# Counting 96-row and 96-column products as full-size ones in a kernel that orders its own work by a clock in the source

## The chip, the cores and the metric

The kernel runs on one core of a Trainium2 chip. Its time is the device time of one launch in microseconds (us), as the median of several runs; lower is better. Short names for engines: PE is TensorE (matmul), PEld its weight loads, DVE is VectorE, ACT is ScalarE, POOL is GpSimd, SP is SyncE, which here only starts DMAs.

## The reference

For x of 2048 tokens and 576 channels, the output is g * a + (1 - g) * b. Here g is a sigmoid of x times a gate vector, a is a long convolution (a state-space layer of 128 states for each channel), and b is a mixture of 4096 tiny experts chosen by product keys in 32 heads:

```python
P = jnp.exp(logdA[:, :, None] * l[None, None, :])
K = jnp.einsum("dn,dnl,dn->dl", Cc, P, dB).real
...                                    # y = irfft(rfft(u) * rfft(K)) + u * Dskip
q = jnp.einsum("nd,dhc->nhc", xf, w_q)             # 32 heads, 2 x 128
s1 = jnp.einsum("nhd,ed->nhe", q1, k1)             # 64 scores, and s2 alike
i1 = jnp.argsort(-s1, axis=-1)[..., :K]            # best 2 of 64, and i2 alike
...                                    # best 2 of the 4 pairs, softmax g
act = _gelu(jnp.einsum("nd,nhkd->nhk", xf, ue))
out = jnp.einsum("nhk,nhk,nhkd->nd", g, act, ve)
```

## The kernel before

All the work is in one function, `body`, written out as one long stream of instructions. Each engine executes its own instructions in the order in which the source issues them, so that the order of issue is the schedule. Exact f32 products are made of three f16 products (high and low halves).

**The work.** In the first two thirds PE works through 128 *s groups* and 128 *a groups*. An s group (`s{c}_{t}`, c 0 to 7, t 0 to 15) makes 512 scores for 128 tokens in 14 products of 128x512; DVE then searches each of its 8 pieces of 64 scores with MAX8 (`m`) and FIND_INDEX8 (`i`), 16 instructions. An a group (`a{c}_{tb}_{j}`) multiplies 128 experts by 512 tokens in 14 products; ACT or DVE empties it into `go`, which SP stores to `g_d`. The operands are built as it goes: `whl` and `wb` from the query weights and keys, `uhl` and `wrem` of each of 8 expert chunks (loaded as `us` and `ur`), each a scaled copy on ACT or DVE and a remainder on DVE.

Beside these groups other pieces run. `k_front` and `k_gen` build the convolution's kernel in 36 steps, two at a time: `k_front` makes angles on PE, `kP`, as two products with 96 rows (and for every fourth step `k_factors` makes their 96-column operand `wbp`), reduces them to `CS` on ACT or DVE, and takes exponents (`e`, `ex`) and sines on ACT; `k_gen` multiplies them (`Y`, `e` on DVE) and makes the tile `kb` in small products of 32 columns. This is called the k stage; it lasts from about 110 to 600 us. `u_stage1` transforms the tokens in 32 steps: ACT and DVE split `uh`, PE makes `u1`, and SP stores it. Then `products` multiplies the two transforms (`ki`, `ui` loaded; `pr`, `pi` on PE; `tt`, `vf`, `vo` on DVE, ACT and POOL; `pv` on PE), `v_work` splits the experts' second matrix into `vhl`, `gating` turns the searches into weights, and `prep` spreads them over experts by one-hot products (`A`, `Be`, `Bg`, then `S`) into the weight tile `wh`. From about 1017 us on PE makes the output tiles `o` from `wh` and `vhl`, 192 products for each of 16 token tiles.

**What sets the order.** The source keeps a count of time of its own while it issues, `clock[0]`. Only `mm` and waiting advance it. Each side piece is a Python generator that yields how long it wants to wait; `pump` resumes those that are due by the count, between PE's groups and every third product inside one. An object for each of DVE, ACT and POOL (`V`, `S`, `G`) adds up when that engine will be free by estimated durations; `rdy` keeps when each tile will be ready. The count of PE's time stands in `mm` (lines 206 to 213):

```python
    def mm(o, l, r, start, stop, cost=None):
        m = l.shape[0], size(l)
        if m != tiling[0]:
            tiling[0] = m
            clock[0] += 0.15 if m == (128, 128) else 0.1
        clock[0] += (size(r) * (4 if r.dtype == F32 else 1) / 2400 + 0.003) if cost is None else cost
```

`m` is the shape of the stationary operand: rows (the contraction) and columns. The count is read in many places. The main loop (line 1534 on) chooses between the next s group and the next a group by how far DVE is behind:

```python
        lag = V.free - clock[0]
        ...
        a_ok = a_ok and (len(acts) > 26 or not groups)
        ...
        if groups and bank_free() and lag < (6.0 if not a_ok else 2.0 if not turn_s else 5.0 if kdone[0] < NCK else 8.0):
```

The last 26 a groups are held back until no s group is left. `k_front` chooses ACT or DVE for each reduction of kP by `S.free <= V.free` (lines 709 and 718 on), `act_post` for each emptying of an a group by `S.free <= V.free + 0.5`. `u_build` (line 1184) starts to load an expert chunk c once `adone[0]`, the a chunks done, has reached c, or c - 1 while the k stage runs or the s groups are not near their end:

```python
        while adone[0] < c - (kdone[0] < NCK or sdone[0] >= 7):
```

In the profile nearly all instructions of DVE, ACT and POOL have line 133 (the engine object), DMAs have line 204 and matmuls line 213, so that one goes by the names of the tiles.

## Time and profile before

| | |
|---|---|
| median of 3 runs | 1479.43 us (1478.44 to 1482.02) |
| profiled execution: time, and span | 1478.13 us, 1476.3 us |
| mean granted clock of PE | 0.995 |
| PE busy | 1434.3 us, 97% |
| DVE / ACT / POOL busy | 1254.2 / 786.0 / 537.7 us |
| chain that ended last | PE 73%, DVE 19%, DMA 3% |

Busy time is the union of an engine's instructions. A chain is followed back from the last instruction, at each step to what released it. PE is nearly always busy, so what is read below is where it is not, and who released it there.

### The profile page before, as it was taken

To read this page: it belongs to the slowest core of one execution; us is meant where nothing else is said; L and a number is where in the kernel's file an instruction comes from. 1 tells how busy PE (TensorE), PEld (TensorE's weight loads), DVE (VectorE), ACT (ScalarE), POOL (GpSimd) and SP (SyncE) were. 2 spreads that over 40 slices of the span, in tenths; PEclk is the share of its full clock that TensorE was granted. 3 is DMA by queue.
4 is the path that set the end of the run, shared out by engine and by line. 5 is a ranking of instruction groups with operands and counts; after the bars stand their busy time and mean duration, and the time that the engine had idled before them with its cause. 6 is when DMAs were issued, how large, how long until landed. Compare 5 with 4: busy or idle time off the path is not lost.

```text
span 1476.3 us, 36780 instructions
## 1 busy us (share of the span) xinstructions
PE 1434.3 (97%) x14024; PEld 861.1 (58%) x14028; DVE 1254.2 (85%) x4589; ACT 786.0 (53%) x1310; POOL 537.7 (36%) x513
## 2 busy tenths in 40 slices
PE   5999999999999999999999999999999999999999
PEld 3444544454455544555554444456787788788787
DVE  6989899989988899598997997589998998898860
ACT  6558778677686866625655644664424324323310
POOL 0454663634726465202247999522010110110100
PEclk9999999999999999999999999999999999999999
DMA  6443542443344343466576758676532442442400
GB/s 227 133 121 103 173 129 76 151 134 94 107 130 147 108 133 122 132 218 234 177 269 228 267 192 258 208 245 186 191 119 92 131 144 70 151 146 67 154 9 17
DMA packets 139184, 221.20 MB, mean 150 GB/s; under 512 B 11648, under 2 KB 82688, under 8 KB 132608
## 3 DMA queue, kind: packets, MB, share of 16 engines
q1 hardware_dynamic: 138912, 218.78, 46.2%
q8 instruction: 110, 1.80, 0.5%
q14 instruction: 66, 0.54, 0.1%
q10 hardware_dynamic: 96, 0.07, 0.0%
HBM read 147.51 MB, written 71.30 MB: 148 GB/s over the span
## 4 chain that ended last, share of the span: by engine, by line
PE 73%; DVE 19%; DMA 3%; ACT 2%; issue 2%; SPq 0%; POOL 0%; DVEq 0%; ACTq 0%
PE o L213 23%; PE a L213 19%; PE s L213 17%; DVE i L133 4%; PE S L213 4%; DVE m L133 3%; PE wb L213 2%; DVE e L133 2%; PE kb L213 2%; DVE uhl L133 2%; PE pr L213 1%; DVE Y L133 1%; DVE CS L133 1%; PE y L213 1%; DVE uh L133 1%
## 5 line engine op out<-in xcount | busy, mean ns | idle before, releaser
L213 PE MATMUL o<-vhl,wh 128*128 128x288 f16 x3072 | 387.3, 286 | 0.0
L213 PE MATMUL s<-whl,xb 128*128 128x512 f16 x1536 | 366.4, 381 | 5.9 <-DVE whl L133 3.5
L213 PE MATMUL a<-xb,uhl 128*128 128x512 f16 x1536 | 362.4, 380 | 4.1 <-DVE i L133 4.1
L213 PEld LDWEIGHTS <-wh 128*128 128x128 f16 x3072 | 295.9, 98 | 76.4 <-issue 3.7
L213 PEld LDWEIGHTS <-xb 128*128 128x128 f16 x1792 | 171.4, 98 | 211.4 <-issue 20.8
L213 PEld LDWEIGHTS <-uhl 128*128 128x128 f16 x1536 | 147.9, 98 | 178.7 <-issue 5.7
L133 DVE FIND_INDEX8 i<-m,s 128x8 uint32<-128x64 f32 x1024 | 206.5, 223 | 0.0
L133 ACT ACTIVATE wh<-gl,s_wg 128x1024 f16<-128x1024 f32 x63 | 67.6, 1137 | 206.8 <-DVE gl L133 206.8
L133 DVE MAX8 m<-s 128x8 f32<-128x64 f32 x1024 | 146.3, 215 | 24.6 <-PE s L213 23.3
L133 POOL TENSOR_TENSOR CS<-CS,ex 128x512 f32<-128x512 f32 x72 | 100.6, 1427 | 153.5 <-DVE ex L133 144.3
L133 POOL TENSOR_TENSOR ya<-ya,db 128x576 f32<-128x576 f32 x16 | 31.8, 1994 | 341.2 <-DVE Bg L133 151.2
L133 DVE SCALAR_TENSOR_TENSOR wh<-gl,s_wg,wh 128x1024 f16<-128x1024 f32 x64 | 90.6, 1447 | 11.3 <-ACT wh L133 11.3
L133 DVE TENSOR_TENSOR gl<-S,gl 128x256 f32<-128x256 f32 x256 | 90.0, 415 | 10.2 <-PE S L213 9.2
L133 POOL TENSOR_TENSOR e<-aN,rt 128x512 f32<-128x512 f32 x72 | 86.4, 1221 | 31.8 <-PE kb L213 31.7
L133 ACT ACTIVATE go<-a,i_a 128x512 f32<-128x512 f32 x95 | 64.4, 683 | 52.1 <-PE a L213 35.2
L133 DVE TENSOR_TENSOR Bg<-Be,vals 128x1024 f16<-128x1024 f16 x128 | 89.6, 741 | 2.2
L133 ACT ACTIVATE gl<-gl 128x1024 f32<-128x1024 f32 x64 | 63.5, 1045 | 44.8 <-DMA gl<-g_d 41.4
L133 DVE TENSOR_TENSOR A<-iota_a,vals 128x2048 f16<-128x2048 f16 x64 | 79.9, 1249 | 0.0
L213 PE MATMUL s<-wrem,xb 128*128 128x512 f16 x256 | 76.7, 381 | 0.1
L213 PE MATMUL a<-xb,wrem 128*128 128x512 f16 x256 | 76.2, 379 | 0.0
L213 PE MATMUL S<-Bg,A 128*128 128x64 f16 x2048 | 73.1, 193 | 2.6 <-DVE Bg L133 2.4
L213 PEld LDWEIGHTS <-A 128*128 128x128 f16 x2048 | 70.8, 97 | 7.7 <-issue 1.8
(202 smaller groups left out, 2225.2 us busy)
## 6 DMA issues: line engine op xcount, KB each, us to landing
g_d<-go SPq DMA_DIRECT2D x128, 256.0 KB, 2.5
gl<-g_d SPq DMA_DIRECT2D x32, 1024.0 KB, 5.7
wq<-in_wq_dram SPq DMA_DIRECT2D x16, 1152.0 KB, 7.1
us<-in_au_dram SPq DMA_DIRECT2D x64, 144.0 KB, 3.0
su_d<-us SPq DMA_DIRECT2D x32, 288.0 KB, 2.7
sk_d<-k1o SPq DMA_DIRECT2D x32, 288.0 KB, 3.0
vn<-in_vv_dram SPq DMA_DIRECT2D x32, 288.0 KB, 3.2
ui<-su_d SPq DMA_DIRECT2D x16, 576.0 KB, 4.2
```

The source lines that it names most:

```text
L133: return f(*a, **k)
L213: T.matmul(o, l, r, start=start, stop=stop)
```

## The change

`mm` counts a change of tiling only between classes: over 64 rows or not, and over 64 columns taken as 128. Products of 96 rows (kP) and of 96 columns (wbp) are so taken as full size. The charge for a return to full size goes from 0.15 to 0.13. No instruction's operands, shape or engine is named in it.

```diff
     def mm(o, l, r, start, stop, cost=None):
-        m = l.shape[0], size(l)
+        m = l.shape[0] > 64, 128 if size(l) > 64 else size(l)
         if m != tiling[0]:
             tiling[0] = m
-            clock[0] += 0.15 if m == (128, 128) else 0.1
+            clock[0] += 0.13 if m == (True, 128) else 0.1
```

PE has the same 11612 matmul instructions in both programs; their order differs from the first kP on. Two places are shown; a row is an instruction, its line, operation, written and read tiles (with buffer numbers), and shape.

On DVE, around the fifth pair of kb (about 230 us), before has both remainders uh9 and uh10 and the remainder of chunk 3 between the searches of score groups s1_8 and s1_9:

```order
L133 MAX_INDEX i8_1_8_2842<-m8_1_8_2841,s1_8_2818 128x8 x8
L133 TENSOR_TENSOR Y9_2866<-e9_2378,CS9_2383 128x1024
L133 TENSOR_TENSOR e9_2378<-e9_2378,CS9_2383 128x16x32
L133 SCALAR_TENSOR_TENSOR e9_2378<-e9_2378,CS9_2383 128x16x32
L133 COPY ex8_2348<-ex8_2348 128x2
L133 COPY ex9_2379<-ex9_2379 128x2
L133 SCALAR_TENSOR_TENSOR uh9_2760<-us_1119,sci_76,uh9_2760 64x576
L133 SCALAR_TENSOR_TENSOR uh10_2787<-us_1119,sci_76,uh10_2787 64x576
L133 SCALAR_TENSOR_TENSOR uhl3_2592<-us3_2469,sci_76,uhl3_2592 128x512
L133 MAX m8_1_8_2841<-s1_9_2926 128x8 x8
```

and now:

```order
L133 MAX m8_1_8_2910<-s1_10_2943 128x8 x8
L133 MAX_INDEX i8_1_8_2911<-m8_1_8_2910,s1_10_2943 128x8 x8
L133 TENSOR_TENSOR Y10_3074<-e10_2634,CS10_2639 128x1024
L133 TENSOR_TENSOR e10_2634<-e10_2634,CS10_2639 128x16x32
L133 SCALAR_TENSOR_TENSOR e10_2634<-e10_2634,CS10_2639 128x16x32
L133 TENSOR_TENSOR Y11_3078<-e11_2669,CS11_2674 128x1024
L133 TENSOR_TENSOR e11_2669<-e11_2669,CS11_2674 128x16x32
L133 SCALAR_TENSOR_TENSOR e11_2669<-e11_2669,CS11_2674 128x16x32
L133 COPY ex10_2635<-ex10_2635 128x2
L133 COPY ex11_2670<-ex11_2670 128x2
L133 SCALAR_TENSOR_TENSOR uh9_2894<-us_1119,sci_76,uh9_2894 64x576
L133 SCALAR_TENSOR_TENSOR uh10_2904<-us_1119,sci_76,uh10_2904 64x576
```

uh9 and uh10 moved behind the searches of s1_9 and s1_10 and behind the products of the k steps 10 and 11, a pair of steps later.

On SP, before loads expert chunk 7 (us7, ur7) among the loads of `products`:

```order
L204 DMA ki5_10478<-sk_d_67 128x1152
L204 DMA vn32_10546<-in_au_dram 32x576 x4
L204 DMA z_d_69<-vo2_10437 128x1152
L204 DMA us7_10627<-in_uT_dram 128x4x512
L204 DMA ur7_10628<-in_uT_dram 64x512 x2
L204 DMA vn33_10636<-in_au_dram 32x576 x4
L204 DMA ui6_10665<-su_d_66 128x1152
```

and now at the end of the k stage, ahead of the last store of a chunk 5:

```order
L204 DMA su_d_66<-us_1119 32x4x576
L204 DMA g_d_65<-go5_3_2_7455 128x4x128
L204 DMA us7_7469<-in_uT_dram 128x4x512
L204 DMA ur7_7470<-in_uT_dram 64x512 x2
L204 DMA g_d_65<-go5_3_3_7478 128x4x128
L204 DMA k_d_68<-ko_7580 128x1024
L204 DMA wq4_1_7655<-in_wq_dram 128x2304
L204 DMA ksb_7665<-k_d_68 128x18x256
L204 DMA g_d_65<-go6_0_0_7700 128x4x128
L204 DMA g_d_65<-go6_0_1_7721 128x4x128
L204 DMA g_d_65<-go6_0_2_7747 128x4x128
```

The load moved some 94 places up; behind it, ahead of the products, stand stores of a chunk 6 (go6_0_0 and on): six a groups of chunk 6 come there now that stood behind the last s group before. So 26 a groups are left behind the last s group, s7_15, where before had 31.

## The prediction
> **What bounds the kernel now.** I read the page first, then busy time by stretches, then the stretches where TensorE (PE) stands still.

> ```profile
> span 1476.3 us, 36780 instructions
> PE 1434.3 (97%) x14024; PEld 861.1 (58%) x14028; DVE 1254.2 (85%) x4589; ACT 786.0 (53%) x1310; POOL 537.7 (36%) x513
> ```

> PE is busy for 1434.3 of 1476.3 us, so 42.0 us is all that an order could bring, plus what the slowed clock costs; and the change leaves PE's products as they are. The windows say where those 42 us lie. The columns are the window, its length, busy time of PE, PE's weight loads, VectorE (DVE), ScalarE (ACT) and GpSimd (POOL), then granted clock, DMA share and GB/s.

> ```profile
> core 0: us, PE busy (x) PEld busy (x) DVE busy (x) ACT busy (x) POOL busy (x), PEclk, DMA share, GB/s
> 200.00:280.00 80.00, 72.84 (x701) 36.85 (x700) 78.75 (x305) 53.21 (x83) 49.56 (x36) 0.98 0.43 131
> 280.00:400.00 120.00, 118.61 (x1287) 61.41 (x1286) 109.18 (x465) 88.50 (x131) 62.14 (x51) 1.00 0.38 116
> 400.00:480.00 80.00, 79.77 (x747) 40.98 (x746) 68.64 (x269) 59.42 (x91) 38.08 (x34) 1.00 0.42 131
> 480.00:560.00 80.00, 80.00 (x741) 39.86 (x740) 73.00 (x270) 62.08 (x88) 41.10 (x33) 1.00 0.42 126
> 560.00:640.00 80.00, 77.38 (x907) 41.02 (x905) 63.45 (x286) 47.85 (x79) 29.87 (x25) 1.00 0.47 150
> 800.00:910.00 110.00, 107.61 (x983) 51.06 (x980) 98.69 (x529) 56.53 (x150) 105.30 (x108) 0.98 0.73 240
> 214.24:217.66 3.42, 3.05 (x108) 2.81 (x111) 3.39 (x5) 0.00 (x0) 3.42 (x3) 0.50 0.56 151
> 849.12:852.54 3.42, 3.42 (x18) 1.19 (x10) 3.42 (x19) 1.66 (x4) 3.34 (x4) 0.50 0.84 275
> ```

> From 200 to 280 us PE stands still for 80.00 - 72.84 = 7.16 us while DVE has 78.75 of 80: DVE sets the pace there. From 280 to 640 it stands for 1.39 + 0.23 + 0.00 + 2.62 = 4.24, from 800 to 910 for 2.39. Two stretches of 3.42 us have a granted clock of 0.50; each costs at most half its length, 1.7 us. The timeline (start, duration, instruction, and in brackets PE's wait and who ended it) shows what the waits are:

> ```profile
> 214.19 0.44 PE L213 MATMUL kb<-Y,CS 128*32 128x64 f32 x8 [2.71 <-DVE i L133]
> 254.15 0.41 PE L213 MATMUL u<-uh,tu 128*128 128x288 f16 x2 [1.79 <-DVE uh L133]
> 255.90 0.41 PE L213 MATMUL u<-uh,tu 128*128 128x288 f16 x2 [0.66 <-DVE uh L133]
> 273.17 0.59 PE L213 MATMUL a<-xb,uhl 128*128 128x512 f16 x2 [1.62 <-DVE i L133]
> 584.13 0.39 PE L213 MATMUL a<-xb,uhl 128*128 128x512 f16 x1 [2.51 <-DVE i L133]
> 848.30 0.43 PE L213 MATMUL pi<-ui,cst 64*64 64x256 f32 x2 [1.60 <-DVE m L133]
> ```

> All six end on DVE; the four of 200 to 280 are 2.71 + 1.79 + 0.66 + 1.62 = 6.78 of the 7.16. PE reached an instruction whose operand or bank was still behind other work in DVE's queue. That is what an order can shift.

> **The change part by part.** *The count itself.* A count inside the source runs no engine; only the order that it sets can act. By the order, 60 products or groups enter a tiling of 96 rows or columns in before (51 of kP, 9 of wb): 60 x 0.1 = 6.0 us of count go, with 43 returns x 0.15 = 6.5; the 86 other returns fall by 0.02, 1.7 together. The count ends up 14.2 us shorter, nearly all of it while kP runs. Does the chip charge what was taken out?

> ```profile
> 281.67 0.81 PE L213 MATMUL s<-whl,xb 128*128 128x512 f16 x3
> 282.41 0.32 PE L213 MATMUL kb<-Y,CS 128*32 128x64 f32 x8
> 285.51 2.11 PE L213 MATMUL s<-whl,xb 128*128 128x512 f16 x9
> 287.45 0.60 PE L213 MATMUL kP<-rt,wb 96*128 96x512 bf16 x2
> 287.89 0.38 PE L213 MATMUL s<-whl,xb 128*128 128x512 f16 x1
> L213 PE MATMUL kP<-rt,wb x72: 377/381/390, 110.6 to 590.5; 96*128 96x512 bf16 x72
> ```

> Nine s products take 287.45 - 285.51 = 1.94, 0.216 each; the two kP products between the same neighbours take 287.89 - 287.45 = 0.44, 0.22 each: nothing for 96 rows. Into kb (32 columns) the three s products take 0.74 where 3 x 0.216 is 0.65: 0.09 for a real switch. So the new count is nearer to the chip. Real switches fall from 172 to 170 in the order: 2 x 0.09, under 0.2 us; I put 0.

> *k stage, 110 to 640 us.* With a shorter count DVE looks further behind PE, so what asks for DVE's lag (which of s and a goes next, whether ACT or DVE reduces a kP or empties an a) turns from DVE to ACT, and side work comes due after more matmuls. I counted each operation in the two orders between the first and the sixth pair of kb and priced it by DVE's groups of 110 to 640 us (count, busy us, mean ns):

> ```profile
> L133 DVE SCALAR_TENSOR_TENSOR uh<-us,sci,uh 64x576 f16<-64x576 f32 x32 | 44.7, 1413 | 1.5 <-ACT uh L133 0.8
> L133 DVE SCALAR_TENSOR_TENSOR CS<-CS,kP 128x512 f32<-128x512 f32 x49 | 32.6, 679 | 2.0 <-ACT CS L133 1.7
> L133 DVE TENSOR_SCALAR go<-a,i_a 128x512 f32<-128x512 f32 x25 | 18.3, 744 | 8.7 <-PE a L213 8.6
> L133 DVE TENSOR_TENSOR CS<-CS,kP 128x512 f32<-128x512 f32 x23 | 15.8, 687 | 0.8
> L133 DVE TENSOR_SCALAR CS<-kP 128x512 f32<-128x512 f32 x23 | 15.7, 683 | 6.4 <-PE kP L213 6.4
> L133 DVE TENSOR_SCALAR whl<-wb,sci 128x512 f16<-128x512 f32 x9 | 6.5, 745 | 7.4 <-PE wb L213 7.4
> ```

> and the short searches by the timeline, where they overlap (8 MAX8 in 1.15 us; a FIND_INDEX8 every 0.20):

> ```profile
> 227.64 1.15 DVE L133 MAX8 m<-s 128x8 f32<-128x64 f32 x8
> 228.76 0.24 DVE L133 FIND_INDEX8 i<-m,s 128x8 uint32<-128x64 f32 x1
> 228.96 0.23 DVE L133 FIND_INDEX8 i<-m,s 128x8 uint32<-128x64 f32 x1
> ```

> uh 10 to 8: -2 x 1.41 = -2.8. kP reduced on DVE alone 7 to 5, with ACT's help 13 to 15: -2 x (0.683 + 0.687) + 2 x 0.679 = -1.4. whl 3 to 0, at the 0.745 of its group: -2.2. go 4 to 3: -0.7. MAX8 8 and FIND_INDEX8 7 more: 1.15 + 7 x 0.20 = +2.6. Together -4.5, and with the groups too small to list -4.9. PE's own work between these marks, by its rows' spacing, is 121.7 us before and 120.7 after; DVE's is 122.0 and 117.1. So DVE goes from 0.3 over PE to 3.6 under. I take 4.5 of the 7.16, short of all since a single late operand still stops PE when the sums fit (bounds 0 and 7.2). The slow clock at 214 begins at the end of the 2.71 us wait; 1.2 of its 1.7 goes with it (bounds 0 and 1.7). For 280 to 640, where DVE has slack, I take 2.5 of 4.24: DVE's rows up to the 28th kb fall from 476.4 to 457.1 against PE's 494.1 to 485.5, 10.7 us more room, but at 584 a single hand-over is late and that can come back elsewhere (bounds 0 and 4.2).

> *Products, 800 to 910 us.* The load of expert chunk 7 stands earlier in SP's queue and its split moves out of here, into the end of the k stage:

> ```profile
> L133 DVE TENSOR_TENSOR tt<-tt 128x512 f32<-128x512 f32 x7 | 10.1, 1448 | 0.5
> L133 DVE SCALAR_TENSOR_TENSOR vhl<-vhl,sci,vhl 128x576 f16<-128x576 f32 x8 | 9.0, 1173 | 0.0
> L133 DVE SCALAR_TENSOR_TENSOR uhl<-us,sci,uhl 128x512 f16<-128x512 f32 x4 | 5.2, 1290 | 0.0
> L133 DVE SCALAR_TENSOR_TENSOR wrem<-ur,sci,wrem 64x512 f16<-64x512 f32 x1 | 1.2, 1202 | 0.0
> ```

> The four uhl and the wrem, 5.2 + 1.2 = 6.4 us of DVE, leave. Between the tenth and the nineteenth pr vhl also goes from 8 to 4 (-4.7), and two more each of the tt sums and vf products come in, 2 x (1.448 + 1.026) = +4.9; copies out of PSUM go to ACT and gating steps come in for about as much. By the order DVE's work there goes from 4.0 us over PE's (45.9 to 41.9) to 0.6 under (40.1 to 40.7). I take 2.8 of the 4.1 there (2.39 standing still, 1.7 slow clock; bounds 0 and 4.1). The load passes one store of a and, further on, the ui, ki and vn loads; a chunk of that size behind a store delays only that store, and three go buffers lie behind it: 0.

> *The tail up to the first o.* Six a groups go ahead of the products, so fewer are left behind the last s: 26 for 31.

> ```profile
> 896.35 0.59 PE L213 MATMUL s<-wrem,xb 128*128 128x512 f16 x2
> 1011.10 1.28 DVE L133 SCALAR_TENSOR_TENSOR wh<-gl,s_wg,wh 128x1024 f16<-128x1024 f32 x1
> 1017.63 1.63 PE L213 MATMUL o<-vhl,wh 128*128 128x288 f16 x12
> 896.90:1017.63 120.73, 119.64 (x1020) 59.37 (x1017) 90.70 (x179) 72.65 (x138) 57.03 (x59) 1.00 0.71 225
> ```

> The weights of the first o are written at 1011.10 + 1.28 = 1012.4, 5.2 us before PE takes them. PE's work from the last s to that o falls from 117.7 to 104.8 by the order, 12.9 us, the same work having been done earlier. If the chain of gates, S and wh were of fixed length, PE would stand for 12.9 - 5.2 = 7.7 us. But its steps on PE lie behind those same a groups, and DVE and ACT lose the groups' emptying too, so the chain shortens with them; I take +1.0 (bounds 0 and +7.7).

> *Sum.* -4.5 - 1.2 - 2.5 - 2.8 + 1.0 = -10.0 on the profiled 1478.13 gives 1468.1. The median of the runs shown stands 1.30 above that run: **1469.4 us**. All gains whole and no loss: -17.2, so 1462.2.

> **The rivals.**

> *The waits only move: no change, 1479.4 us, 0.18.* For: the same products and nearly the same DVE work in all (1253 us of rows to 1245); a count that ends earlier is no chip time. Against: the balance changes just where DVE is full.

> *Slower: 1487.1 us, 0.20.* The chain to the first o is bound by latency, not by PE; with 12.9 us less cover the full 7.7 us of standing is paid and the k stage only swaps one late operand for another. For: 5.2 us is all the room that before shows, and PE is busy for 119.64 of 120.73 there only because of the a groups. It decides the sign once the gains above it are under 7.7 - 4.4 = 3.3 us.

> *The clock is not tied to these waits: 1472.3 us, 0.10.* Both slowed stretches are 3.42 us long, the one at 214.24 right behind a wait of 2.71, the other behind one of 1.60; waits of 1.62 at 273 and 2.51 at 584 have none behind them. So the clock may drop by chance of phase, and stay when the wait goes: then 1.2 and 1.7 of the gains are lost, 1469.4 + 2.9. [...]

> *All of it: 1462.2 us, 0.07.* Every wait of 200 to 640 and 800 to 910 goes with both slowed stretches.

> **How the numbers follow.** The forecast itself has 0.45. Runs of this kernel tell a difference of about 0.3%, 4.4 us, from none. Faster by more: 0.45 + 0.10 + 0.07 = 0.62; within: 0.18; slower: 0.20. The range goes from all gains at the low end, 1462, to the slower rival at the high end, 1487; beyond lie perhaps half of that rival and of the best case, 0.14. The gains' own range, which holds most of the chance, is 1462 to 1475.

> **What would show it.** In after's profile: under 3 us of PE standing still in the 80 us that hold the third to sixth kb, with DVE below its 98% there; no standing of 1.6 us before a pi; the first o within 6 us of wh's last write, with under 2 us of standing before it. Wrong would be: waits of PE on DVE of the same sum in 200 to 640 at other products (rival one), or over 5 us between the last a group and the first o (rival two).

## The result, and the profile after

The changed kernel takes 1470.16 us, median of 6 runs (1466.87 to 1474.96), against 1480.46 (1478.44 to 1483.74) for the kernel before on the same chip: a ratio of 0.993, with a 95% interval of 0.991 to 0.995. It is faster by 0.7%, clear of the 0.3% that the prediction takes as the least to be told. The forecast was 1469.4.

The page of after:

```profile
span 1464.8 us, 36792 instructions
PE 1430.1 (98%) x14024; PEld 858.5 (59%) x14028; DVE 1251.1 (85%) x4568; ACT 798.8 (55%) x1337; POOL 531.0 (36%) x508
```

PE's idle time falls from 42.0 to 1464.8 - 1430.1 = 34.7 us. The windows of after, cut as before:

```profile
200.00:280.00 80.00, 80.00 (x863) 40.56 (x862) 76.30 (x307) 56.09 (x84) 50.73 (x40) 1.00 0.43 130
280.00:400.00 120.00, 118.69 (x1169) 60.65 (x1168) 104.64 (x357) 95.80 (x139) 62.50 (x53) 1.00 0.40 124
400.00:480.00 80.00, 80.00 (x802) 40.76 (x801) 74.11 (x284) 62.12 (x95) 43.19 (x33) 1.00 0.49 147
480.00:560.00 80.00, 78.84 (x798) 40.37 (x797) 67.78 (x222) 60.64 (x87) 43.98 (x37) 1.00 0.40 120
560.00:640.00 80.00, 80.00 (x780) 41.03 (x779) 65.31 (x370) 40.31 (x67) 16.83 (x16) 1.00 0.60 181
800.00:910.00 110.00, 108.31 (x1047) 51.30 (x1040) 95.36 (x540) 57.30 (x161) 106.19 (x110) 1.00 0.70 234
900.00:1100.00 200.00, 193.70 (x2038) 124.78 (x2037) 173.22 (x272) 104.03 (x169) 67.50 (x62) 1.00 0.60 196
```

and the last of them in before, which was not shown:

```profile
900.00:1100.00 200.00, 195.99 (x1956) 121.28 (x1948) 166.95 (x276) 97.44 (x160) 65.11 (x62) 1.00 0.64 202
```

From 200 to 280 us nothing is left of the 7.16 us in which PE stood still, and DVE has fallen from 78.75 to 76.30. From 280 to 640 it is 1.31 + 0.00 + 1.16 + 0.00 = 2.47, where it was 4.24. From 800 to 910 it is 1.69 for 2.39, and the clock is 1.00. Only from 900 to 1100 does PE stand longer, 6.30 for 4.01 us. The profiled run of after, 1466.87 us, is the lowest of its six. The waits of after by what ended them, from 110 to 900 us, those of 0.5 us or more (total, times, longest), and the largest single one behind that:

```profile
PE a L213 <- issue: 1.4, 2, 0.8
PE u L213 <- ACT us L133: 1.3, 1, 1.3
PE pi L213 <- DVE m L133: 0.9, 1, 0.9
PE pv L213 <- DVE m L133: 0.7, 1, 0.7
```

```profile
1037.39 0.20 PE L213 MATMUL S<-Bg,A 128*128 128x64 f16 x1 [2.51 <-DVE Bg L133]
```

None of the six waits shown of before is left at its length; the one of pi is 0.9 for 1.60.

### The profile page after: what moved, and what is told of

The parts are those of the page before. It is cut to its first block, busy times and chain, and to the rows that moved or that the text cites. A ratio compares the mean times of both kernels' runs of the same rounds, so it can differ in the third digit from the quotient of the medians.

```text
span 1464.8 us, 36792 instructions
## 1 busy us (share of the span) xinstructions
PE 1430.1 (98%) x14024; PEld 858.5 (59%) x14028; DVE 1251.1 (85%) x4568; ACT 798.8 (55%) x1337; POOL 531.0 (36%) x508
## 4 chain that ended last, share of the span: by engine, by line
PE 81%; DVE 8%; POOL 3%; ACT 3%; DMA 3%; issue 2%; SPq 0%; ACTq 0%; POOLq 0%; DVEq 0%
PE o L213 23%; PE a L213 22%; PE s L213 21%; PE S L213 4%; PE kb L213 2%; PE wb L213 2%; POOL vf L133 2%; PE u L213 1%; PE kP L213 1%; DMA xs<-in_xT_dram 1%; PE pr L213 1%; PE y L213 1%; POOL tt L133 1%; PE k L213 1%; DVE wh L133 1%
## 5 line engine op out<-in xcount | busy, mean ns | idle before, releaser
L213 PE MATMUL o<-vhl,wh 128*128 128x288 f16 x3072 | 387.1, 286 | 0.0
L213 PE MATMUL s<-whl,xb 128*128 128x512 f16 x1536 | 368.0, 380 | 4.7 <-DVE whl L133 3.5
L213 PE MATMUL a<-xb,uhl 128*128 128x512 f16 x1536 | 361.2, 379 | 1.8 <-issue 1.4
L213 PEld LDWEIGHTS <-wh 128*128 128x128 f16 x3072 | 296.0, 98 | 76.5 <-issue 3.7
L213 PEld LDWEIGHTS <-xb 128*128 128x128 f16 x1792 | 171.7, 98 | 209.2 <-issue 18.3
L213 PEld LDWEIGHTS <-uhl 128*128 128x128 f16 x1536 | 147.5, 98 | 175.5 <-issue 4.8
L133 DVE FIND_INDEX8 i<-m,s 128x8 uint32<-128x64 f32 x1024 | 206.5, 222 | 0.0
L133 ACT ACTIVATE wh<-gl,s_wg 128x1024 f16<-128x1024 f32 x64 | 68.8, 1137 | 203.0 <-DVE gl L133 203.0
L133 DVE MAX8 m<-s 128x8 f32<-128x64 f32 x1024 | 146.3, 215 | 23.9 <-PE s L213 23.2
L133 POOL TENSOR_TENSOR CS<-CS,ex 128x512 f32<-128x512 f32 x72 | 100.1, 1423 | 148.1 <-DVE ex L133 148.1
L133 POOL TENSOR_TENSOR ya<-ya,db 128x576 f32<-128x576 f32 x16 | 32.0, 2013 | 309.9 <-DMA ya<-in_au_dram 107.4
L133 ACT ACTIVATE go<-a,i_a 128x512 f32<-128x512 f32 x95 | 64.7, 684 | 74.4 <-PE a L213 61.2
L133 DVE SCALAR_TENSOR_TENSOR wh<-gl,s_wg,wh 128x1024 f16<-128x1024 f32 x62 | 91.4, 1504 | 11.3 <-ACT wh L133 11.3
L133 DVE TENSOR_TENSOR gl<-S,gl 128x256 f32<-128x256 f32 x256 | 90.2, 415 | 9.8 <-PE S L213 9.2
L133 POOL TENSOR_TENSOR e<-aN,rt 128x512 f32<-128x512 f32 x72 | 83.8, 1184 | 39.4 <-PE kb L213 39.3
L133 DVE TENSOR_TENSOR Bg<-Be,vals 128x1024 f16<-128x1024 f16 x128 | 89.8, 743 | 2.2
L133 ACT ACTIVATE gl<-gl 128x1024 f32<-128x1024 f32 x64 | 63.3, 1044 | 35.2 <-DMA gl<-g_d 35.1
L213 PE MATMUL S<-Bg,A 128*128 128x64 f16 x2048 | 73.1, 193 | 6.3 <-DVE Bg L133 6.1
L133 DVE TENSOR_TENSOR A<-iota_a,vals 128x2048 f16<-128x2048 f16 x64 | 77.8, 1216 | 0.0
L213 PEld LDWEIGHTS <-A 128*128 128x128 f16 x2048 | 70.8, 97 | 11.8 <-issue 4.6
L213 PE MATMUL s<-wrem,xb 128*128 128x512 f16 x256 | 76.2, 379 | 1.4 <-DVE xb L133 1.3
L213 PE MATMUL a<-xb,wrem 128*128 128x512 f16 x256 | 76.2, 379 | 0.0
```

The lines of the kernel that those rows point to most:

```text
L133: return f(*a, **k)
L213: T.matmul(o, l, r, start=start, stop=stop)
```

## The experiments

Twelve kernels ran. Ratios are to the kernel before on the same chip, with the 95% interval; the changed kernel has 0.993 (0.991 to 0.995).

**The two halves of the change.**

```diff
-        m = l.shape[0], size(l)
+        m = l.shape[0] > 64, 128 if size(l) > 64 else size(l)
...
-            clock[0] += 0.15 if m == (128, 128) else 0.1
+            clock[0] += 0.15 if m == (True, 128) else 0.1
```

> Only the classes (96 rows or columns count as full size); the return charge stays 0.15. The order is that of the changed kernel up to the second pair of kb and nearly so to the sixth: between the third and sixth pair DVE has 70.2 us of work to PE's 72.0, the same as the changed kernel (before: 77.1 to 71.4). Theory A (PE stands still in the k stage where DVE's queued work is over PE's): under 1.5 us of standing between 200 and 280 us and no slow clock there; the nine products between the tenth and nineteenth pr have DVE 3.7 under PE, so under 1.5 us of standing by 800 to 910; about 1471 us. Rival B (any new order trades single late operands, whatever the balance): several us of standing on DVE somewhere in 200 to 640, and a time anywhere from 1470 to 1486.

Measured: 1484.81 us, 1.0053 (1.0039 to 1.0066), slower than before. The windows of 200 to 280 us and of the one long stop:

```profile
200.00:280.00 80.00, 80.00 (x863) 40.70 (x862) 75.88 (x305) 55.88 (x84) 50.45 (x41) 1.00 0.43 130
492.80:510.40 17.60, 0.03 (x1) 0.00 (x0) 17.19 (x22) 17.50 (x23) 10.44 (x10) 0.56 0.46 150
```

The timeline of PE in it:

```profile
510.49 1.12 PE L213 MATMUL u<-uh,tu 128*128 128x288 f16 x4 [17.66 <-DVE uh L133]
```

Theory A holds at its place (no standing from 200 to 280) and the time missed all the same: PE came to a u whose uh stood behind 16 us of other work in DVE's queue. DVE is busy for 17.19 of the 17.60 us in which PE does nothing, and ACT for 17.50, so it is the order of the queues and no missing transfer. ACT's own copy of uh, which DVE's remainder needs, came late too, from 503.66 to 504.42; DVE's step ran from 508.41 to 510.34. That one stop is worth more than all that the change gains. By the order DVE had about as much work as PE there, which the expectation had not looked at. The time is in rival B's range, and so is the kind of stop.

```diff
-            clock[0] += 0.15 if m == (128, 128) else 0.1
+            clock[0] += 0.13 if m == (128, 128) else 0.1
```

> Only the return charge goes from 0.15 to 0.13; 96 rows and columns count as changes, as before. Its order leaves that of the kernel before at the first kP. DVE has 64.6 us to PE's 65.3 between the third and sixth pair of kb, and 64.1 to 72.7 in the next three. Theory A: under 2 us of standing between 200 and 280 us, so about 1471 us. PE's work behind the last s is 90.1 us where before had 117.7 and the changed kernel 104.6. Rival C (the chain to the first o has a length of its own, 97 us as in the changed kernel's trace): PE stands 7 us before the first o and the time is about 1478 us; by A's reading of the tail (the chain shortens with its load) under 2 us there. Rival B: 1470 to 1486, with no relation to the balance.

Measured: 1475.38 us, 0.9982 (0.9973 to 0.9991). PE stood 4.06 us from 200 to 280, 3.27 from 800 to 910, and not at all from 910 to 1030: no wait before the first o with 90.1 us of cover. Rival C is out; theory A's 2 us was too low by half, and its 1471 us by 4: a balance just under PE (64.6 to 65.3) did not keep PE going.

Each half alone gives +0.5% and -0.2%, both together -0.7%: the parts do not add, since each draws another order.

**Where along the kernel the gain is.** The new count is used only from the sixth pair of kb on, or only up to it.

```diff
+        new = kdone[0] >= 12        # the other kernel: kdone[0] < 12
```

> The old count until six pairs of kb are issued (about 275 us), the new count from then on. The order up to there is that of the kernel before: DVE 77.1 us to PE's 71.4 between the third and sixth pair. Theory A: the 7 us of standing between 200 and 280 us stay, with the slowed clock at 214, so at best about 1478 us. If the gain came from what lies behind (the expert chunk loaded earlier, fewer DVE steps later): about 1472 us, with the early standing still there. Rival B: 1470 to 1486.

Measured: 1470.93 us, 0.9956 (0.9943 to 0.9969). The early standing stayed, as its window shows:

```profile
200.00:280.00 80.00, 74.04 (x701) 36.94 (x700) 78.75 (x305) 53.49 (x82) 49.58 (x36) 0.96 0.43 129
```

80.00 - 74.04 = 5.96 us, and the clock lower than before's 0.98. But the time is 7 us below what A allowed, and near the 1472 forecast for a gain that lies behind: PE stood 0.07 + 0.35 us from 910 to 1100 where before had 4.0, 0 from 280 to 400 for 1.39, 0.88 from 800 to 910 for 2.39, though 4.97 from 400 to 640 for 2.85. So there is as much to gain behind 280 us as ahead of it.

> The new count until six pairs of kb are issued, the old count (with 96 rows and 0.15) from then on. To the sixth pair the order is the changed kernel's (DVE 70.2 to PE's 72.0); behind it DVE stays under PE in every stretch of the k stage (the closest is 66.4 to 67.2) and PE has 93.1 us behind the last s. Theory A: no standing between 200 and 280 us, under 2 us from 280 to 640, under 1.5 from 800 to 910; with the tail as in the run with the new count from the sixth pair on (0.4 us between 910 and 1100): about 1464 us, below the changed kernel. Rival B: a time anywhere from 1470 to 1486. Rival C (tail of a length of its own): 1470 or above with the standing before the first o.

Measured: 1466.64 us, 0.991 (0.9897 to 0.9924). No standing from 200 to 280, 1.71 from 280 to 640, 1.19 from 800 to 910, 2.24 from 910 to 1100. Its one larger stop is 2.7 us at 701, with a slowed clock behind it, for k1o; the time is 2.6 us above theory A's 1464, and below what rivals B and C allowed.

**DVE's work as the cause of the 200 to 280 us waits.** In the changed kernel's own order, Y is made twice in six k steps:

```diff
             V.tensor_mul(Y..., ev, CS[:, :, 1:2, :]...)
+            if 4 <= d < 10:             # the other kernel: 14 <= d < 20
+                nc.vector.tensor_mul(Y..., ev, CS[:, :, 1:2, :]...)
```

> The changed kernel in its own order, in which DVE makes the product Y of six k steps (4 to 9, about 175 to 250 us) a second time: 6 x 1.37 = 8.2 us more of DVE work, not counted by the source, so that nothing else moves. DVE goes to 78.4 us against PE's 72.0 between the third and sixth pair of kb (before: 77.1 to 71.4). Theory A (the sum of DVE's work there sets the pace): PE stands 5 to 8 us on DVE between 175 and 290 us where it stood 0, and the time is 5 to 9 us above the changed kernel's, about 1477 us. Rival B (single operands placed late in the order are what stops PE; the order is the changed one, so none is): under 2 us more, about 1472 us.

> The same 8.2 us of doubled Y, but in k steps 14 to 19 (about 290 to 360 us), where DVE in the changed kernel has 72.2 us of work to PE's 84.1 in the next three pairs of kb. Theory A: it stays under PE, so at most 1.5 us more of standing, about 1471 us. Rival B': any delay of an operand costs, wherever it is: 5 us or more, 1475 us or above.

Measured: 1476.63 us, 0.9981 (0.997 to 0.9993), and 1473.2 us, 0.9952 (0.9936 to 0.9968). The window of the kernel with the extra work in the tight place:

```profile
200.00:280.00 80.00, 76.26 (x724) 37.75 (x722) 78.60 (x294) 50.82 (x77) 48.52 (x38) 1.00 0.42 124
```

and of the one with it in the slack place:

```profile
280.00:400.00 120.00, 117.48 (x1155) 59.73 (x1154) 107.96 (x331) 91.96 (x134) 64.13 (x54) 0.99 0.39 118
```

In the tight place 3.74 us of standing, and 1.04 in the 40 us ahead of it, where the changed kernel has none: 4.8 us for 8.2 us of work, and half a per cent of the time. In the slack place 2.52 for 1.31: 1.2 us. Theory A had 5 to 8 us for the first, 0.2 more than came, and at most 1.5 for the second; rival B's 2 us or less for the first is out. The second time is above its forecast by 2 us, about half way to the 1475 of rival B' (any delay costs); a slowed stretch behind a 2.0 us wait is part of it, and its interval overlaps with that of the changed kernel.

In the order of before, the other way:

```diff
-            V.scalar_tensor_tensor(ev[:, :, 1], ev[:, :, 1], -1.0, CS[:, :, 3], ...)
+            if not 4 <= d < 10:         # else only counted in V.free
+                V.scalar_tensor_tensor(ev[:, :, 1], ev[:, :, 1], -1.0, CS[:, :, 3], ...)
```

> The kernel before in its own order, in which one DVE product of e is left out in k steps 4 to 9 (the second half of e isn't multiplied by CS there, so the convolution's kernel is not the reference's), while the source still counts it: 6 x 0.9 = 5.4 us less of DVE work and nothing moved. DVE has 72 us to PE's 71.4 there. Theory A: PE's standing between 200 and 280 us falls from 7.2 to about 2 us, and the slowed clock at 214 goes with the 2.7 us wait: about 1472 us. Rival B: the late operands stand where they stood, 5 us or more of standing stays: 1477 us or above.

Measured: 1477.35 us, 0.9983 (0.9973 to 0.9992). The window:

```profile
200.00:280.00 80.00, 74.85 (x712) 37.55 (x710) 76.94 (x307) 54.43 (x84) 49.27 (x36) 0.98 0.43 132
```

and its waits for kb:

```profile
PE kb L213 <- DVE i L133: 1.8, 1, 1.8
PE kb L213 <- POOL CS L133: 1.3, 1, 1.3
```

Only 2.0 of the 7.2 us went, for 5.4 us of work. kb waits 0.9 us less for DVE, but 1.3 for POOL's CS, 0.9 more than before; the waits of u for uh fall from 2.45 to 0.5 us; the wait of a at 273 stays at 1.63, and so does the slowed stretch behind kb's wait. Theory A alone would have taken 5. What came is rival B's forecast: 5.15 us of standing, and 1477 us. So DVE's sum is one part of it; the other is which operand stands where, and the change moved both.

**The products.** In the order of before, DVE's five steps on expert chunk 7 go to ACT as plain copies.

```diff
+        V.mute = dst_lo.tensor.name.startswith('uhl7')      # counted, not issued
         V.scalar_tensor_tensor(dst_lo, src, s, dst_hi, ...)
+        if V.mute:
+            nc.scalar.activation(dst_lo, src, AF.Copy, scale=s)
```

> The kernel before in its own order; DVE's five steps on expert chunk 7 (four uhl and one wrem, 5.2 + 1.2 us, about 820 to 860 us) are replaced by plain copies on ACT (the low half of that chunk is not the reference's) and still counted on DVE. Theory: the wait of 1.60 us of pi at 848 goes, and with it the slowed stretch behind it (1.7 us): 800 to 910 has 1 us of standing or less and a clock of 1.00; 3 us below before, about 1477 us. Rival (pi's wait was for a bank behind the searches, chunk 7 is only beside it): the wait stays, 1479 us or above.

Measured: 1477.07 us, 0.9982 (0.9969 to 0.9995). The window:

```profile
800.00:910.00 110.00, 108.33 (x1039) 51.73 (x1030) 95.26 (x548) 60.65 (x159) 106.78 (x111) 1.00 0.76 251
```

and the wait that came in:

```profile
PE pv L213 <- ACT tt L133: 1.5, 1, 1.5
```

pi no longer waits and the clock is 1.00; a pv waits 1.5 us for ACT in its place, so 1.67 us of standing are left, not 1 or less; 0.7 us of it and the slowed stretch are what is gained. The sum is that of the changed kernel there (1.69 us, clock 1.00), where the waits left are on DVE; ACT's five added copies may have brought the wait of pv, which was not tested.

**The tail.** Five more a groups held back in the changed kernel:

```diff
-        a_ok = a_ok and (len(acts) > 26 or not groups)
+        a_ok = a_ok and (len(acts) > 31 or not groups)
```

> The changed kernel with 31 in place of 26 a groups held back for the end. The order is that of the changed kernel up to the seventeenth pair of kb; behind the last s PE has 118.8 us of work in place of 104.6. Theory A with the tail's price: PE's standing at S on DVE between 900 and 1100 us (5.7 us in the changed kernel, 2.4 before) falls to about 2.4, so about 1467 us. Rival: those stops are DVE's own queue between two o tiles and have nothing to do with the groups held back; they stay, 1470 us, or more if the end of the k stage loses.

Measured: 1476.5 us, 0.9986 (0.9974 to 0.9999). The waits of S for Bg did fall, from 5.7 to 3.3 us between 900 and 1100, not to 2.4, but the end of the k stage, which gave the groups up, stood 5.91 us from 560 to 640 with a clock of 0.96. Its waits there:

```profile
PE wn L213 <- ACT wj L133: 4.6, 2, 3.5
PE s L213 <- DVE whl L133: 1.3, 1, 1.3
```

The a groups had been the cover for building whl; taken from there, that wait comes up. DVE's rows ahead of the 2.51 us wait in the changed kernel show what stood before it:

```profile
1022.33 1.97 DVE L133 SCALAR_TENSOR_TENSOR vhl<-vhl,sci,vhl 128x576 f16<-128x576 f32 x1
1024.23 2.43 DVE L133 SCALAR_TENSOR_TENSOR wh<-gl,s_wg,wh 128x1024 f16<-128x1024 f32 x1
1026.58 0.81 DVE L133 SCALAR_TENSOR_TENSOR vhl<-vs,sci,vhl 128x576 f16<-128x576 f32 x1
...
1030.73 1.97 DVE L133 SCALAR_TENSOR_TENSOR vhl<-vs,sci,vhl 128x576 f16<-128x576 f32 x1
...
1036.64 1.29 DVE L133 TENSOR_TENSOR Bg<-Be,vals 128x1024 f16<-128x1024 f16 x2
```

Three vhl steps, 1.97 + 0.81 + 1.97 = 4.75 us, stand ahead of Bg. Before has none between 1020 and 1049. With the last two chunks' steps on ACT as plain copies:

```diff
+                        V.mute = c >= 6                     # counted, not issued
                         V.scalar_tensor_tensor(h[:, j, 1, :], x, sv[0], h[:, j, 0, :], ...)
+                        if c >= 6:
+                            nc.scalar.activation(h[:, j, 1, :], x, AF.Copy, scale=sv[0])
```

> The changed kernel in its own order; the remainders of the last two chunks of v that DVE makes (four steps, 0.8 to 2.0 us each, about 6 us, between 1000 and 1035 us) are replaced by plain copies on ACT, so that the low half of these chunks is not the reference's; the source counts them on DVE as before, and nothing else moves. Theory (the vhl steps that left the products came back here, ahead of A, Be and Bg in DVE's queue): the wait of 2.51 us of S at 1037 goes, PE's standing on Bg between 900 and 1100 falls from 5.7 to 3 us or less, and the time is 2 to 4 us below the changed kernel's, about 1467 us. Rival (S waits for its own chain A, Be, Bg and gl, whatever else is queued): 5 us or more stays, 1470 us.

Measured: 1465.65 us, 0.990 (0.9883 to 0.9918). The wait at 1037 is gone; the window:

```profile
900.00:1100.00 200.00, 196.21 (x2062) 126.57 (x2062) 171.37 (x276) 109.41 (x176) 66.72 (x62) 1.00 0.61 199
```

and its waits for Bg there:

```profile
PE S L213 <- DVE Bg L133: 3.3, 5, 1.2
```

3.79 us of standing for 6.30. S waits 3.3 us, a little over the 3 expected, since the two smaller waits ahead of the vhl steps stay. The interval of the time overlaps with that of the changed kernel, so that it is the trace that decides here. The expectation's remark that these steps had left the products does not hold, as is shown below.

**Other orders.**

```diff
-            clock[0] += 0.13 if m == (True, 128) else 0.1
+            clock[0] += 0.14 if m == (True, 128) else 0.1
```

> The changed kernel with 0.14 in place of 0.13 for a return to full size, the nearest neighbour. To the sixth pair of kb the order is the changed kernel's; DVE is level with PE between the sixteenth and twenty-second kb (73.4 to 73.3) and among the products (55.1 to 55.2), and the tail has 95.4 us. Theory A: no standing between 200 and 280, 1 to 3 us in each of the two level stretches, under 2 in the tail: about 1470 us. Rival B (0.13 is one draw among many, each order with its own late operands): anywhere from 1466 to 1486, with a stop that the balance does not name.

Measured: 1468.59 us, 0.992 (0.9907 to 0.9933), the changed kernel's time within the intervals. The two stretches where DVE is level came out at 0 (400 to 560) and 3.19 us (800 to 910); 3.00 us stood from 640 to 800, mostly for k1o, which the balance does not name. So 0.13 is no special value, but 0.15 with the same classes gives 1484.81: one more hundredth of a microsecond for each return puts one u ahead of its operand.

The kernel with the new count up to the sixth pair of kb, and six buffers for k1o:

```diff
-            o = fk.tile([128, D], F32, tag="s1o", name=f"k1o{w}", bufs=4)
+            o = fk.tile([128, D], F32, tag="s1o", name=f"k1o{w}", bufs=6)
```

> The run with the new count until the sixth pair of kb, with six buffers for k1o in place of four; the order is the same. There PE stood 2.7 us behind ACT's k1o at 701 us and its clock was slowed behind that; ACT itself had stood 4.35 us for the store of an earlier k1o. Theory (ACT and DVE wait there for a buffer that SP's queue is late to store): the 2.7 us and the slowed stretch (1.7 us) go: about 1462 us. Rival (the store is late, so the next load or bank waits in its place): 1466 us.

Measured: 1463.75 us, 0.989 (0.9876 to 0.9905), below both kernels. With four buffers, PE's and ACT's wait on the timeline:

```profile
701.35 0.65 PE L215 MATMUL k<-ksb,tk 128*128 128x288 f16 x4 [1.90 <-ACT k1o L133]
700.89 0.41 ACT L133 ACTIVATE k1o<-k 128x288 f32<-128x288 f32 x1 [4.35 <-DMA sk_d<-k1o]
```

With six, PE's waits from 640 to 800 us:

```profile
PE wn L215 <- ACT wj L133: 1.1, 1, 1.1
PE s L215 <- ACT k1o L133: 0.3, 1, 0.3
```

The 2.7 us for k1o are down to 0.3 and no slowed stretch is left between 110 us and the last o; 1.1 us come up elsewhere, so 2.9 of the 4.4 us are had (1466.64 to 1463.75). The two intervals just touch (0.9897 to 0.9924, and 0.9876 to 0.9905); the traces have the same sum, 1.3 us less of standing there and 1.7 of slowed clock.

## Why the prediction came out

The time was right by 0.8 us and the sign was right, but the terms of the sum are off in both directions, so that so close a sum is luck. Three of the four signs named for it came: no standing where the third to sixth kb are, with DVE busy for 95%, no wait of 1.6 us before a pi, and under 2 us of standing ahead of the first o; the fourth is answered under the tail. From the profiled run of before (span 1476.3) to that of after (1464.8) are 11.5 us; the terms below measure -7.2 - 1.7 - 1.8 - 2.4 + 2.3 = -10.8 of them. The medians differ by 10.3.

- **200 to 280 us:** forecast -4.5 with bounds 0 and -7.2; measured -7.2, all of it. The slowed clock at 214: forecast -1.2; 1.7 went. The caution that a single late operand still stops PE was right (with 5.4 us of DVE work left out of before, 5.15 us of standing stays), but the change moved those operands as well. That the order up to the sixth pair is what took the waits away is shown across the kernels: the eight profiles with the new order there and no work added to it have no standing from 200 to 280, the four with the old one 5.15 to 7.16 us. That DVE's work is a cause is shown by the doubled Y; that it is the only one is refuted by the run with less of it.
- **280 to 640 us:** forecast -2.5; measured 4.24 to 2.47, -1.8. The wait at 584 went; others of 1.3 and 1.2 came.
- **Products:** forecast -2.8; measured -0.7 of standing and -1.7 of slowed clock, -2.4. The cause named, chunk 7's steps on DVE, is shown for the wait of pi by giving them to ACT in before alone.
- **The tail:** forecast +1.0; measured +2.3 between 900 and 1100, and not at the place named. PE does not wait at the first o, and 0.93 us at the S just ahead of it:

```profile
994.49 2.47 DVE L133 SCALAR_TENSOR_TENSOR wh<-gl,s_wg,wh 128x1024 f16<-128x1024 f32 x2
...
1004.17 1.10 PE L213 MATMUL S<-Bg,A 128*128 128x64 f16 x31 [0.93 <-DVE Bg L133]
1005.11 0.59 PE L213 MATMUL a<-xb,wrem 128*128 128x512 f16 x2
1005.54 0.65 PE L213 MATMUL o<-vhl,wh 128*128 128x288 f16 x4
```

The last wh that DVE writes ahead of it ends at 994.49 + 2.47 = 996.96, 8.6 us earlier, where before had 5.2: with less cover the room grew, so that the sign "within 6 us" failed in the harmless direction. With 90.1 us of cover there was no wait before it either. So the second rival's mechanism, a chain of fixed length, is refuted, and the +1.0 had the wrong reason.

The step that failed is that the tail was priced only up to the first o; what DVE would still have to do behind it was put at nothing. The waits of PE from 900 to 1100 in before:

```profile
PE S L213 <- DVE Bg L133: 1.6, 2, 1.3
PE y L213 <- DMA tf<-in_tf_dram: 1.2, 1, 1.2
PE pr L213 <- DMA ki<-sk_d: 1.1, 1, 1.1
```

and after:

```profile
PE S L213 <- DVE Bg L133: 5.7, 5, 2.5
PE tr L213 <- ACT vo L133: 0.4, 1, 0.4
```

So 2.3 us of waits for DMA went and 4.1 came at S. DVE's vhl steps (window, length, busy time and count, then clock, DMA share and GB/s) in before:

```profile
800.00:910.00 110.00, 9.00 (x8) 0.98 0.73 240
900.00:1000.00 100.00, 10.51 (x12) 1.00 0.72 226
1020.00:1049.00 29.00, 0.00 (x0) 1.00 0.76 237
```

and after:

```profile
800.00:910.00 110.00, 9.78 (x8) 1.00 0.70 234
900.00:1000.00 100.00, 10.40 (x10) 1.00 0.71 240
1020.00:1049.00 29.00, 4.74 (x3) 1.00 0.64 217
```

The three steps did not come from the products, where DVE makes eight in both kernels; the four that the prediction has leaving the stretch between the tenth and the nineteenth pr only run a little earlier, from 810 us on. In before the last vhl step ends at 1003.97, 13.7 us ahead of the first o. After, the first o starts 12.1 us earlier, and the last steps, of the last chunks of v, fall behind it, between the o tiles where S waits for Bg. With the last four steps taken from DVE, 2.5 us went.

- **No switch price for 96 rows:** this stands by the rows of before (0.22 us for a kP product with 96 rows, 0.216 for an s product), but it does not explain the gain. The halves give +0.5% and -0.2%, a return charge of 0.14 gives the same as 0.13, one of 0.15 is slower than before, and the new count over only part of the kernel is as good as all of it within the intervals. A count nearer to the chip is not shown to make a better order: six orders from counts that differ by a tenth of a microsecond or less for a step (before apart) lie between 1466.64 and 1484.81 us. That the gain of this one was to be had from its order is shown; that another such change would gain is not.
- **The first rival, waits only move:** it did not hold as a whole, but did in part: 2.3 us came back in the tail and 2.5 us at other products between 280 and 640.
- **The third rival, slowed stretches that stay:** refuted in its form. In all fourteen profiles, from 110 us to the last o, no slowed stretch stands without a wait of PE of 1.6 us or more directly ahead of it or around it. But such a wait does not always bring one: 17 of 33 waits of 1.5 us or more did. The rival was right in that phase plays a part: the last section shows one wait of 2.51 us with no slowed stretch behind it in before, and the same wait with one in another run.

## What to carry to other kernels

Where a count in the source sets the order, a small change of the count is a draw of a new order; read the order for places where PE reaches an operand that stands behind a long stretch of another engine's queue, since one such place (17.7 us here) outweighs several stages of better balance. Where an order lets a later stage start sooner, look for what then still stands in the queues behind that start: compare the counts of each operation, stretch by stretch, over the whole program. When an order is good, look at its largest remaining wait for a cause outside the order, such as too few buffers: two more of k1o gave 2.9 us here, with PE's order the same.

## What the runs showed of the hardware

PE's clock fell to one half behind waits of 1.6 to 3.5 us (and in the one of 17.66), in stretches of 3.41 us or twice that (in the run with chunk 7's steps on ACT the clock is 0.61 from 215 to 220 us and 0.71 from 220 to 225, which is 6.8 us at one half), and not at each of them. The same wait, in the same order, at 584 us in before:

```profile
584.13 2.76 PE L213 MATMUL a<-xb,uhl 128*128 128x512 f16 x12 [2.51 <-DVE i L133]
```

and in the run with six products of e left out, where it comes 1 us earlier:

```profile
583.13 4.45 PE L213 MATMUL a<-xb,uhl 128*128 128x512 f16 x12 [2.51 <-DVE i L133]
```

```profile
579.47:582.88 3.41, 2.16 (x12) 0.98 (x10) 3.41 (x18) 1.13 (x2) 2.04 (x3) 1.00 0.26 77
582.88:586.29 3.41, 2.16 (x10) 1.00 (x11) 3.41 (x23) 0.00 (x0) 3.41 (x3) 1.00 0.47 154
```

and on that of the other run:

```profile
580.58:583.99 3.41, 0.90 (x7) 0.41 (x5) 3.41 (x25) 0.69 (x1) 3.41 (x3) 1.00 0.26 77
583.99:587.40 3.41, 3.41 (x9) 1.18 (x8) 3.34 (x29) 0.00 (x0) 3.41 (x5) 0.50 0.21 77
```

In before the wait lies across two steps, 1.25 us in each, and the clock stays at 1.00; in the other run all 2.51 us lie in one step, and the next has a clock of 0.50: the 12 products behind the wait take 4.45 us where they took 2.76, 1.7 us on top of the 2.5. In the fourteen profiles, from 110 us to the last o, every step of such a grid in which PE stood for 1.99 us or more had a slowed one behind it; of 16 others with 1.5 us or more 3 did, and none with less began a slowed stretch. Why those 3 did and the other 13 did not stays open. Of the 17 waits that brought a slowed stretch 15 were under 2.8 us, less than a whole step of 3.41. So in these profiles a wait of PE cost its length and, where 2 us or more of it fell into one step, about 1.7 us more, an estimate from the 12 products above: 13 of the 16 waits of 1.9 us or more brought a slowed stretch, and 4 of the 17 shorter ones.
